# A spectral filter and an MLP in one kernel: the first DFT stage of batches 2 to 7 on quarters of the TensorE array

## The chip, the cores and the metric

The kernel runs on one core of a Trainium2 chip. The core has five engines that run side by side and wait for each other by semaphores: PE (TensorE, matmuls; PEld is its loading of weights), DVE (VectorE), ACT (ScalarE), POOL (GpSimd) and SP (SyncE, here used only to issue DMAs). Matmul results land in PSUM, which has eight banks of 128 partitions x 512 fp32 values; ACT and DVE copy them out to SBUF ("evacuate" them). The metric is the device time of one execution in microseconds (us); lower is better.

## The reference

Two operators follow each other. The first filters each of 8 batches of 3008 rows x 256 channels in the frequency domain; the second is an MLP with the snake activation.

```python
X = np.fft.rfft(x, axis=1)
F = (filt_r + 1j * filt_i)[None, :, :]
y = np.fft.irfft(X * F, n=x.shape[1], axis=1)
...
h = y.reshape(B * S, D) @ w_in          # 24064 x 256 by 256 x 2048
s = np.sin(alpha * h)
g = h + s * s / (alpha + 1e-09)
out = g @ w_out                         # 2048 x 256
```

## The kernel before, in words

**The transform.** 3008 = 47 x 64. The row index is split as n = 64 n1 + n2 with n1 < 47 and n2 < 64, and the DFT is made in two matmul stages, with their inverses behind. The first stage (`first`, tile pa) is a DFT of length 47 over n1: for each n2, 47 rows of x are contracted into 24 frequencies s, real and imaginary, thus 48 outputs. Since one such matmul would fill little of the 128x128 array, two are laid together: the chunk of x has 94 partitions, 47 values of n1 by two halves h of n2, and the weight table `wf_t` (94 x 96) is block-structured with the same 47x48 table for both halves and zeros between. A chunk `ch` holds 8 values of n2 in each half and all 256 channels; one matmul (L181) takes two of them, 512 columns. So a batch has 4 chunks of 4 matmuls. Each writes its own PSUM tile pa, which is copied as fp16 into `t1_h` (L184, by `evac`); after a chunk's fourth copy a DMA on SP's queue writes the 96 rows to DRAM (tile d1, L186).

Behind it, `load_t2` reads d1 back with n2 and the real and imaginary part on the partitions (tile t, POOL's queue), `forward` (tile pb) makes the second DFT, ACT copies it to xf, SP's queue makes a copy xs with its halves exchanged, DVE multiplies by the filter (`product`, `cross`: tiles p and xs), `inverse` (tile pc) goes back, its result g is written to DRAM (d2), read back (t4) and `last` (tile pd) yields y. Batch 0 goes by another path ahead of the main loop; batches 1 to 7 go by this one.

**The MLP.** The main loop runs over 48 chunks of up to 512 rows of y, each in 8 steps. In a step `hidden` makes two tiles ph (two accumulating matmuls each, L541). ACT takes the cosine of each (L545), DVE combines cosine and ph into v (L546). `project` then contracts the v of the chunk before with w_out, 8 matmuls of 256 columns (tile po, L560), and ACT copies po out (L568).

**The order is written out by hand.** Every piece of the transform of batch b is put into a list with a place in steps (`put(at, ...)`, where z = 48 b), the list is sorted, and `slot` calls the pieces that have come due between the step's two ph and its eight po, or after the po. Pieces with matmuls (pe=True) are spread: one per slot, unless they are late. Each engine works through its instructions in the order in which they were issued.

**PSUM.** Three pools share the eight banks: `fps` (2 banks, tag "f") serves pa, pb, pc and pd; `hps` (4 banks, tag "h") serves ph; `ops` (2 banks) serves po. A new tile waits for the evacuation of what lay in its bank before. For ph, that is DVE's v.

**evac.** `flip` counts evacuations modulo 3; without a given engine two of three go to ACT (L160) and one to DVE (L162).

**Loads of x.** `load_x` puts a chunk of x with one DMA on POOL's queue into one of four buffers (L141); it converts fp32 to fp16 on the way. From batch 2 on it also waits for the latest v (`marks["snake"]`).

Lines by tile, as the profile names them: pa L181, pb L201, pc L232, pd L254 (L343 for batch 0), ph L541, po L560, cosine L545, v L546, copies by ACT L160 and by DVE L162, xs and p L221, L215 and L222, g the copies of pc. L366 (`inverse_table`) builds a table at the start with transposes that write 64 of the 128 partitions in turn: lhsT has 64 columns there. L292, L377 and L431 belong to the start too.

Of the kernel before, what the change touches and what calls it, by code (L numbers as in the profile page):

```python
# [9 lines left out]
FP16 = mybir.dt.float16  # L10
FP32 = mybir.dt.float32
# [7 lines left out]
B, S, C = 8, 3008, 256  # L19
DFF = 2048  # L20
N1, N2 = 47, 64
NS, NQ = 24, 64
NR = 2 * N1
NK = 4 * NS
FUSED = 1


def dft_tables():

    n1, n2 = np.arange(N1), np.arange(N2)  # L30
    s, q = np.arange(NS), np.arange(NQ)
    ph = 2 * np.pi * np.outer(n1, s) / N1
    w = np.stack([np.cos(ph), -np.sin(ph)], 1)
    wf = np.zeros((N1, 2, 2, NS, 2))
    wi = np.zeros((2, NS, 2, N1, 2))
    v = np.stack([2 * np.cos(ph), -2 * np.sin(ph)], 0)
    v[0, :, 0], v[1, :, 0] = 1.0, 0.0
    for h in range(2):
        wf[:, h, :, :, h] = w
        wi[:, :, h, :, h] = v.transpose(0, 2, 1) * (8.0 / S)  # L40

    kap = np.where(q[:, None] < 32, s + N1 * q[:, None], s + N1 * (95 - q[:, None]))
    sg = np.where(q < 32, 1.0, -1.0)[:, None]
    th = 2 * np.pi * n2[:, None, None] * kap / S
    c, sn = np.cos(th), np.sin(th)
    d = np.zeros((2, N2, NS, 2, NQ))
    d[0, :, :, 0] = c.transpose(0, 2, 1)
    d[1, :, :, 0] = sn.transpose(0, 2, 1)
    d[0, :, :, 1] = (-sn * sg).transpose(0, 2, 1)
    d[1, :, :, 1] = (c * sg).transpose(0, 2, 1)  # L50
    f16 = np.float16
    wf, wi = wf.reshape(N1 * 2, 2, NS, 2), 2 * wi.reshape(2, NS, 2, NR)
    wf0, wi0 = np.zeros((96, 2, 2, 32)), np.zeros((2, 2, 32, NR))
    wf0[:NR, :, :, :NS] = wf.transpose(0, 1, 3, 2)
    wi0[:, :, :NS] = wi.transpose(0, 2, 1, 3)
    d = d.reshape(128, NS, 128).astype(f16)
    e = d.transpose(2, 1, 0) * f16(0.125)
    return (wf.reshape(NR, NK).astype(f16), wi.reshape(NK, NR).astype(f16), d,
            wf0.reshape(96, 128).astype(f16), wi0.reshape(128, NR).astype(f16), e)


# [1 line left out]
def kernel(  # L63
# [8 lines left out]
    out: bass.AP,  # L72
):
    nc = tc.nc
    wf_host, wi_host, d_host, wf0_host, wi0_host, e_host = dft_tables()
    wf_dram = nc.inline_tensor(wf_host, name="wf_tbl")
    wi_dram = nc.inline_tensor(wi_host, name="wi_tbl")
    d_dram = nc.inline_tensor(d_host, name="d_tbl")
# [8 lines left out]
    def after(ins, other):  # L87

        tc.add_manual_dep(ins.ins, other.ins.name, mybir.DependencyInfo(
            mybir.DependencyClass.Sync, mybir.DependencyReason.DATA), reason="order of loads")  # L90

    def pool(name, bufs, space=None):
        kw = {} if space is None else {"space": space}
        return ctx.enter_context(tc.tile_pool(name=name, bufs=bufs, **kw))

    cpool = pool("consts", 1)
    xpool = pool("xp", 4)
# [8 lines left out]
    fps = pool("fps", 2, PSUM)  # L106
    hps = pool("hps", 4, PSUM)
    ops = pool("ops", 2, PSUM)

    wf_t = cpool.tile([NR, NK], FP16)  # L110
    t1_h = [cpool.tile([128, 16, C], FP16, name=f"t1_h{i}") for i in range(2)]
    t4_a = cpool.tile([128, 2, 16, C], FP16)
    t4_h = [t4_a[:, i] for i in range(2)]
# [11 lines left out]
    for h in range(2):  # L125
        nc.sync.dma_start(out=x32[:, 4 * C * h:4 * C * h + 4 * C],
                          in_=bass.AP(tensor=x.tensor, offset=x.offset + 4 * h * C, ap=[[32 * C, 96], [1, 4 * C]]))
# [8 lines left out]
    marks = {}  # L136

    def load_x(b, ch):
        xt = xpool.tile([NR, 8, C], FP16, name=f"x_{b}_{ch}", tag="x")
        for n0, n in [(0, 8)] if b or ch < 3 else [(0, 4), (4, 4)]:  # L140
            ins = nc.gpsimd.dma_start(  # L141
                out=xt[:, n0:n0 + n],
                in_=bass.AP(tensor=x.tensor, offset=x.offset + (b * S + ch * 8 + n0) * C,
                            ap=[[32 * C, NR], [C, n], [1, C]]),
            )
        if b == 0:
            marks["x", ch] = ins
        if b == 1:
            marks["x1", ch] = ins
            after(ins, marks["w_in"])  # L150
        if b > 1:
            after(ins, marks["snake"])
        return xt

    flip = [0]
# [1 line left out]
    def evac(dst, src, on_act=None):  # L157
        flip[0] = (flip[0] + 1) % 3
        if flip[0] if on_act is None else on_act:
            marks["act"] = nc.scalar.copy(out=dst, in_=src)  # L160
        else:
            marks["dve"] = nc.vector.tensor_copy(out=dst, in_=src)  # L162

    class Spectral:

        def __init__(self, b):
# [5 lines left out]
            self.x, self.t2, self.t4, self.xf, self.xs, self.p = {}, {}, {}, {}, {}, {}  # L172
            self.fused = b >= FUSED

        def load_x(self, ch):
            self.x[ch] = load_x(self.b, ch)

        def first(self, i):
            ch, j = divmod(i, 4)
            ps = fps.tile([128, 512], FP32, name=f"pa_{self.b}_{i}", tag="f")  # L180
            marks["pe"] = nc.tensor.matmul(out=ps[0:NK, :], lhsT=wf_t, rhs=self.x[ch][:, 2 * j:2 * j + 2, :],  # L181
                                           start=True, stop=True)
            r0 = 8 * (ch % 2)
            evac(t1_h[ch // 2][0:NK, r0 + 2 * j:r0 + 2 * j + 2, :], ps[0:NK, :])  # L184
            if j == 3:
                nc.sync.dma_start(out=self.d1_rows[:, 8 * ch:8 * ch + 8, :],   # L186
                                  in_=t1_h[ch // 2][0:NK, r0:r0 + 8, :])

        def load_t2(self, g):
            self.t2[g] = t2pool.tile([128, 6, C], FP16, name=f"t2_{self.b}_{g}", tag="t2")  # L190
            for p in range(2):
                a0 = p * NS + 6 * g
                nc.gpsimd.dma_start(out=self.t2[g][64 * p:64 * p + 64, :, :],  # L193
                                    in_=self.d1[a0:a0 + 6, :, :].rearrange("s n c -> n s c"))
# [69 lines left out]
    id32 = cpool.tile([16, 16], FP32)  # L264
    nc.scalar.dma_start(out=id32, in_=id32_dram.ap())

    x0 = [xpool.tile([NR, 8, C], FP16, name="x_0_0", tag="x")] + [load_x(0, ch) for ch in range(1, 4)]
    nc.gpsimd.dma_start(out=d_t, in_=d_dram.ap())
    id16 = cpool.tile([128, 128], FP16)
    nc.gpsimd.dma_start(out=id16, in_=id16_dram.ap())  # L270
# [25 lines left out]
    for g in range(2):  # L296
        gs = slice(12 * g, 12 * g + 12)
        for k, filt in enumerate((filt_r, filt_i)):
            for q in range(2):
                if (g, k, q) == (0, 1, 1):  # L300
# [3 lines left out]
                    out=f_t[k][64 * k + 32 * q:64 * k + 32 * q + 32, gs, :],  # L304
                    in_=bass.AP(tensor=filt.tensor, offset=filt.offset + off,
                                ap=[[N1 * C, 32], [step, 12], [1, C]]))
# [89 lines left out]
    for i in range(16):  # L396
        own, tag = (fps, "f") if i % 3 == 2 else (hps, "h")
        ps = own.tile([128, 512], FP32, name=f"pa_0_{i}", tag=tag)
        nc.tensor.matmul(out=ps, lhsT=wf0_t[0:NR], rhs=x0[i // 4][:, 2 * (i % 4):2 * (i % 4) + 2, :],
                         start=True, stop=True)  # L400
# [62 lines left out]
    for g in range(6):  # L463
        own, tag = (t2pool, "t2") if g < 3 else (gpool, "g")
# [3 lines left out]
        ins = nc.sync.dma_start(out=w_in32[g][1], in_=w_in_v[:, :, js])  # L468
        if g == 0:
            after(ins, marks["filt", 1, 0])  # L470
        marks["w_in"] = ins
    nc.sync.dma_start(out=wf_t, in_=wf_dram.ap())
    nc.sync.dma_start(out=wi_t, in_=wi_dram.ap())
    w_out32 = vpool.tile([128, 16, C], FP32, name="w_out32", tag="v")
    for jb in range(0, 16, 8):
        ins = nc.sync.dma_start(out=w_out32[:, jb:jb + 8],
                                in_=moe_w_out[128 * jb:128 * jb + 1024].rearrange("(b p) c -> p b c", p=128))
# [120 lines left out]
    def put(at, fn, *args, pe=False):  # L598
        pending.append((at, len(pending), pe, fn, args))
# [6 lines left out]
    for b in range(1, B):  # L606
        s = s1 if b == 1 else Spectral(b)
        z = 48 * b
        if b > 1:
            for ch in range(4):  # L610
                put(22 + 4 * ch if b == 2 else z - 92 + 7 * ch, s.load_x, ch)
        for i in range(16):
            put(6.9 + 0.35 * i if b == 1 else 37 + 0.63 * i if b == 2 else z - 67 + 0.66 * i, s.first, i, pe=True)
        for g in range(4):
            put(12.5 if b == 1 else 47 if b == 2 else z - 56, s.load_t2, g)
        for u in range(12):
            inv = 24 + 1.21 * u if b == 1 else 59 + 2.1 * u if b == 2 else z - 40.8 + 2.3 * u
            fwd = inv - (6 if b == 1 else 6)
            put(fwd, s.forward, u, pe=True)
            put(fwd + (0.5 if b == 1 else 1.5), s.product, u)  # L620
            if s.fused:
                put(fwd + (4 if b == 1 else 4.5), s.cross, u)
            put(inv, s.inverse, u, pe=True)
        for ch in range(4):
            put(z - (9.5 if b == 1 and ch < 3 else (10.5, 10.5, 10.5, 3)[ch]), s.load_t4, ch)
        for u in range(16):
            put(z + (u - (5 if b == 1 else 6.5) if u < 4 else 2 * u - 9), s.last, u, pe=True)
# [59 lines left out]
```

## Time and profile before

| what | value |
|---|---|
| three runs | 786.86, 786.45, 785.05 us; median 786.45 |
| the profiled execution's own time | 783.39 us |
| its span, from the first to the last instruction | 781.6 us |
| granted TensorE clock in it | 1.0 |
| DVE L546, v | 768 of 671 ns, 482.8 us busy |
| ACT L545, cosine | 768 of 591 ns, 411.1 us busy |
| PE L560, po | 3008 of 272 ns, 389.4 us busy |
| PE L541, ph | 1536 of 374 ns, 388.0 us busy |
| ACT L160, copies of pa | 77 of 584 ns |
| DVE L162, copies of pa | 35 of 681 ns |
| PEld L181, loads of wf_t | 112 of 123 ns |
| POOL L141, loads of x | 32 issues of 540 ns; 30 of them with 376 KB, 5.0 us to landing |

The first stage of batch 2 lies at 109 to 130 us of the span, that of batch 3 at 187 to 208, then at 282 to 303, 374 to 395, 469 to 490 and 560 to 581. In these six stretches, 129.4 us in all, DVE was busy for 108.5 us and ACT for 105.4.

How to read it: a row gives line, engine, operation, out<-in, shape and count, then busy time and mean length of one, then the engine's idle time ahead of these instructions with what ended it. A matmul's record runs from its start to the modelled arrival of its last result, and the next matmul starts well before that; so records overlap, and the time that a matmul holds the engine is seen in the distance of starts. In the timeline the columns are start, length to the end of the merged group, engine, line and what is done.

### The profile page before, as it was taken

The numbers are of one execution on the slowest core, as the hardware profiler recorded it, in microseconds if no ns is written. First come the engines' busy times: TensorE is split into PE (matmuls) and PEld (weight loads), VectorE is DVE, ScalarE is ACT, GpSimd is POOL, SyncE is SP. The second block draws the span as 40 slices with busy tenths as digits, with TensorE's granted clock in tenths as the row PEclk, the third lists the DMA queues.
The fourth block names the chain that finished last, engine by engine and source line by source line (L and its number), as shares of the span: only waits on it lengthen the run. The fifth ranks groups of instructions, "written<-read, shape, count | busy, mean of one in ns | idle before, by whom it ended". The sixth has DMA issues, their size and how long they took to land.

```text
span 781.6 us, 16646 instructions
## 1 busy us (share of the span) xinstructions
PE 771.7 (99%) x5799; PEld 535.1 (68%) x5799; DVE 653.0 (84%) x1163; ACT 617.7 (79%) x1213; POOL 114.7 (15%) x192
## 2 busy tenths in 40 slices
PE   8999999999999999999999999999999999999997
PEld 4757767676667767676667766766666776766666
DVE  7887997899779997899878998789977899777773
ACT  5798988888878887888878888788887887777664
POOL 6456354200020001100020000200002000000001
PEclk9999999999999999999999999999999999999999
DMA  9946676754655446645474454736465232421111
GB/s 222 284 105 165 142 160 189 160 124 116 195 143 107 112 117 191 149 112 105 134 220 93 106 130 124 222 79 134 102 175 163 68 99 76 122 58 28 41 42 55
DMA packets 86683, 100.99 MB, mean 129 GB/s; under 512 B 14924, under 2 KB 74322, under 8 KB 86600
## 3 DMA queue, kind: packets, MB, share of 16 engines
q1 hardware_dynamic: 74525, 71.01, 32.5%
q0 software_dynamic: 11776, 28.80, 18.5%
q8 instruction: 45, 0.74, 0.4%
q14 instruction: 38, 0.31, 0.1%
q10 hardware_dynamic: 299, 0.13, 0.1%
HBM read 55.72 MB, written 46.66 MB: 131 GB/s over the span
## 4 chain that ended last, share of the span: by engine, by line
PE 94%; DVE 2%; DMA 1%; ACT 1%; issue 1%; POOL 1%; SPq 0%; POOLq 0%; ACTq 0%
PE po L560 41%; PE ph L541 40%; PE pa L181 3%; PE pd L254 2%; PE pb L201 2%; PE pc L232 2%; DVE v L546 1%; DMA id<-id 1%; PE pc L453 1%; PE pb L431 1%; PE pd L343 0%; PE warm L377 0%; POOL x L141 0%; ACT cos_all L545 0%; ACT t_h L160 0%
## 5 line engine op out<-in xcount | busy, mean ns | idle before, releaser
L546 DVE SCALAR_TENSOR_TENSOR v<-cos_all,ph 128x512 f16<-128x512 f32 (+1 forms) x768 | 482.8, 671 | 108.4 <-ACT cos_all L545 105.2
L545 ACT ACTIVATE cos_all<-ph 128x512 f32<-128x512 f32 (+1 forms) x768 | 411.1, 591 | 94.1 <-PE ph L541 93.3
L560 PE MATMUL po<-w,v 128*128 128x256 f16 x3008 | 389.4, 272 | 0.0
L541 PE MATMUL ph<-y,w 128*128 128x512 f16 (+1 forms) x1536 | 388.0, 374 | 0.7 <-DVE v L546 0.6
L560 PEld LDWEIGHTS <-v 128*128 128x128 f16 x3008 | 288.3, 98 | 77.7 <-issue 1.5
L541 PEld LDWEIGHTS <-w 128*128 128x128 f16 x1536 | 147.8, 98 | 104.5 <-issue 3.9
L568 ACT COPY o<-po 128x512 f32<-128x512 f32 (+1 forms) x97 | 55.7, 574 | 20.6 <-PE po L560 14.1
L592 POOL DMA_DIRECT2D out_dram<-o x69 | 36.0, 529 | 209.7 <-ACT o L568 208.9
L193 POOL DMA_DIRECT2D t<-d x56 | 36.4, 662 | 171.7 <-DMA out_dram<-o 131.7
L204 ACT CAST xf<-pb 128x512 f16<-128x512 f32 x84 | 49.8, 593 | 11.8 <-PE pb L201 10.7
L141 POOL DMA_DIRECT2D x<-in_x_dram x32 | 17.2, 540 | 265.9 <-PE pc L232 164.0
L160 ACT CAST t_h<-pa 96x512 f16<-96x512 f32 x77 | 45.0, 584 | 8.4 <-PE pa L181 8.2
L160 ACT CAST y<-pd 128x376 f16<-128x376 f32 (+1 forms) x83 | 39.9, 481 | 8.2 <-PE pd L254 4.4
L254 PEld LDWEIGHTS <-t_a 96*128 96x128 f16 x448 | 31.4, 97 | 18.6 <-issue 0.4
L181 PE MATMUL pa<-x,wf_t 94*96 94x512 f16 x112 | 42.5, 381 | 0.7 <-ACT t_h L160 0.4
L160 ACT CAST g<-pc 128x512 f16<-128x512 f32 x59 | 35.0, 592 | 8.6 <-PE pc L232 8.0
L222 DVE TENSOR_TENSOR p<-p,xs 128x512 f16<-128x512 f16 x84 | 35.7, 425 | 2.9
L254 PE MATMUL pd<-wi_t,t_a 96*128 96x94 f16 x448 | 37.1, 204 | 0.0
L221 DVE TENSOR_TENSOR xs<-xs,filt_t 128x512 f16<-128x512 f16 x84 | 35.0, 417 | 0.5 <-DMA xs<-xf 0.5
L215 DVE TENSOR_TENSOR p<-xf,filt_t 128x512 f16<-128x512 f16 x84 | 35.0, 417 | 0.3 <-PE pc L232 0.3
L201 PE MATMUL pb<-t,d_t 128*128 128x256 f16 x168 | 32.1, 272 | 0.0
L232 PE MATMUL pc<-p,e_t 128*128 128x256 f16 x168 | 32.1, 273 | 0.0
(64 smaller groups left out, 284.4 us busy)
## 6 DMA issues: line engine op xcount, KB each, us to landing
x<-in_x_dram POOLq DMA_DIRECT2D x30, 376.0 KB, 5.0
d<-t_h SPq DMA_DIRECT2D x28, 384.0 KB
t<-d POOLq DMA_DIRECT2D x56, 192.0 KB, 4.4
xs<-xf SPq DMA_DIRECT2D x168, 64.0 KB
d<-g SPq DMA_DIRECT2D x56, 192.0 KB
t_a<-d SPq DMA_DIRECT2D x28, 384.0 KB
out_dram<-o SPq DMA_DIRECT2D x92, 80.0 KB
w_out<-in_moe_w_out_dram SPq DMA_DIRECT2D x2, 1024.0 KB
```

The costliest lines, as they stand in the source:

```text
L160: marks["act"] = nc.scalar.copy(out=dst, in_=src)
L181: marks["pe"] = nc.tensor.matmul(out=ps[0:NK, :], lhsT=wf_t, rhs=self.x[ch][:, 2 * j:2 * j + 2, :], start=True, stop=True)
L193: nc.gpsimd.dma_start(out=self.t2[g][64 * p:64 * p + 64, :, :], in_=self.d1[a0:a0 + 6, :, :].rearrange("s n c -> n s c"))
L201: nc.tensor.matmul(out=ps[:, i, :], lhsT=d_t[:, s, :], rhs=self.t2[s // 6][:, s % 6, :], start=True, stop=True)
L204: nc.scalar.copy(out=self.xf[u], in_=ps)
L232: nc.tensor.matmul(out=ps[:, i, :], lhsT=e_t[:, 2 * w + i, :], rhs=pt[:, i, :], start=(k == 0), stop=(k == len(pr) - 1))
L254: nc.tensor.matmul(out=psv[:, i, :], rhs=wi_t, start=True, stop=True, lhsT=t4_h[ch // 2][0:NK, n0 % 16 + i, cb * 128:cb * 128 + 128])
L541: nc.tensor.matmul(out=ps[:, 0:n], lhsT=w1[:, cb, jb * 128:jb * 128 + 128], rhs=y_cols[:, cb, c0:c0 + n], start=(cb == 0), stop=(cb == 1))
L545: nc.scalar.activation(out=cs[:, 0:n], in_=ps[:, 0:n], func=AFT.Sin, bias=float(np.pi / 2))
L546: marks["snake"] = nc.vector.scalar_tensor_tensor(out=v[k][:, jb, 0:n], in0=cs[:, 0:n], scalar=-1.0, in1=ps[:, 0:n], op0=ALU.add, op1=ALU. ...
L560: nc.tensor.matmul(out=pso[k][:, t % 2, :], lhsT=v[k][:, jb, 128 * t:128 * t + 128], rhs=w2[:, jb, :], start=(jb == 0), stop=(jb == 15))
L568: nc.scalar.copy(out=o[:, i0:t % 2 + 1, :], in_=pso[k][:, i0:t % 2 + 1, :])
```

## The change

Batches 2 to 7 get a new first stage, `first_tiled`; batch 1 keeps `first`. A chunk of x now lies on two groups of partitions, n1 = 0 to 46 of half h = 0 on partitions 0 to 46 and those of h = 1 on 64 to 110, by two DMAs with 47 rows each. The weight table `wt_t` holds the plain 47x48 table twice, at rows 0 and 64, with 64 columns (16 of them zero). A matmul takes 47 rows and 64 columns, a quarter of the array: h picks the half of the rows, c the half of the columns, and so the half of the PSUM partitions that is written. Each still has 512 columns of x (two values of n2, all channels). A chunk has 8 of them instead of 4, in two rounds q of four. The two halves h write different PSUM tiles. The first round takes both banks of `fps`, the second takes two of the four banks of `hps`, which until then served ph alone. The four copies of a chunk now cover all 128 partitions; h = 0 goes to ACT, h = 1 to DVE. Two DMAs on SP's queue write d1 in place of one, with the same content at the same place.

Issue moves too: a whole chunk with its 8 matmuls, 4 copies and 2 DMAs is one piece of the list, where before each of its 4 matmuls was a piece of its own.

```diff
+    wt = np.zeros((2, 64, 64))
+    wt[:, :N1, :2 * NS] = w.reshape(N1, 2 * NS)
...
-        xt = xpool.tile([NR, 8, C], FP16, name=f"x_{b}_{ch}", tag="x")
+        xt = xpool.tile([128, 8, C], FP16, name=f"x_{b}_{ch}", tag="x")
+        if b >= TILED:
+            for h in range(2):
+                ins = nc.gpsimd.dma_start(
+                    out=xt[64 * h:64 * h + N1],
+                    in_=bass.AP(tensor=x.tensor, offset=x.offset + (b * S + 32 * h + ch * 8) * C,
+                                ap=[[64 * C, N1], [1, 8 * C]]))
+                after(ins, marks["snake"])
+            return xt
+        xt = xt[0:NR]
...
+        def first_tiled(self, ch):
+            r0 = 8 * (ch % 2)
+            for q in range(2):
+                own, tag = (hps, "h") if q else (fps, "f")
+                ps = [own.tile([128, 512], FP32, name=f"pa_{self.b}_{ch}_{q}_{h}", tag=tag) for h in range(2)]
+                for h in range(2):
+                    for c in range(2):
+                        n = 4 * c + 2 * q
+                        nc.tensor.matmul(out=ps[h][64 * c:64 * c + 64, :], lhsT=wt_t[64 * h:64 * h + N1],
+                                         rhs=self.x[ch][64 * h:64 * h + N1, n:n + 2, :], start=True, stop=True)
+                for h in range(2):
+                    evac(t1_h[ch // 2][:, r0 + 4 * h + 2 * q:r0 + 4 * h + 2 * q + 2, :], ps[h], h == 0)
+            d1 = self.d1.rearrange("a (h n) c -> a h (n c)", h=2)
+            for c in range(2):
+                n0 = (8 * ch + 4 * c) * C
+                nc.sync.dma_start(out=d1[:, :, n0:n0 + 4 * C],
+                                  in_=t1_h[ch // 2][64 * c:64 * c + 2 * NS, r0:r0 + 8, :]
+                                  .rearrange("a (h n) c -> a h (n c)", h=2))
...
+    nc.sync.dma_start(out=wt_t, in_=wt_dram.ap())
...
-        for i in range(16):
-            put(6.9 + 0.35 * i if b == 1 else 37 + 0.63 * i if b == 2 else z - 67 + 0.66 * i, s.first, i, pe=True)
+        if b < TILED:
+            for i in range(16):
+                put(6.9 + 0.35 * i, s.first, i, pe=True)
+        else:
+            for ch in range(4):
+                put((37, 40, 42, 45)[ch] if b == 2 else z - 67 + (0, 3, 5, 8)[ch], s.first_tiled, ch, pe=True)
```

More of the change, by code (lines that the diff above doesn't have):

```diff
@@ L25 @@
 FUSED = 1
+TILED = 2
 def dft_tables():
@@ L57, in dft_tables @@
     e = d.transpose(2, 1, 0) * f16(0.125)
-    return (wf.reshape(NR, NK).astype(f16), wi.reshape(NK, NR).astype(f16), d,
+    wt = np.zeros((2, 64, 64))
+    wt[:, :N1, :2 * NS] = w.reshape(N1, 2 * NS)
+    return (wt.reshape(128, 64).astype(f16), wf.reshape(NR, NK).astype(f16), wi.reshape(NK, NR).astype(f16), d,
             wf0.reshape(96, 128).astype(f16), wi0.reshape(128, NR).astype(f16), e)
@@ L74 @@
     nc = tc.nc
-    wf_host, wi_host, d_host, wf0_host, wi0_host, e_host = dft_tables()
+    wt_host, wf_host, wi_host, d_host, wf0_host, wi0_host, e_host = dft_tables()
+    wt_dram = nc.inline_tensor(wt_host, name="wt_tbl")
     wf_dram = nc.inline_tensor(wf_host, name="wf_tbl")
@@ L110 @@
     wf_t = cpool.tile([NR, NK], FP16)
+    wt_t = cpool.tile([128, 64], FP16)
     t1_h = [cpool.tile([128, 16, C], FP16, name=f"t1_h{i}") for i in range(2)]
@@ L150, in load_x @@
             after(ins, marks["w_in"])
-        if b > 1:
-            after(ins, marks["snake"])
         return xt
@@ L265 @@
     nc.scalar.dma_start(out=id32, in_=id32_dram.ap())
-    x0 = [xpool.tile([NR, 8, C], FP16, name="x_0_0", tag="x")] + [load_x(0, ch) for ch in range(1, 4)]
+    x0 = [xpool.tile([128, 8, C], FP16, name="x_0_0", tag="x")[0:NR]] + [load_x(0, ch) for ch in range(1, 4)]
     nc.gpsimd.dma_start(out=d_t, in_=d_dram.ap())
```

## The prediction

> **What bounds the kernel now.** I read the page's first lines, then its chain, then the rows of the engines that meet in this stage.
>
> ```profile
> span 781.6 us, 16646 instructions
> PE 771.7 (99%) x5799; PEld 535.1 (68%) x5799; DVE 653.0 (84%) x1163; ACT 617.7 (79%) x1213; POOL 114.7 (15%) x192
> ...
> PE 94%; DVE 2%; DMA 1%; ACT 1%; issue 1%; POOL 1%; SPq 0%; POOLq 0%; ACTq 0%
> ...
> L181 PE MATMUL pa<-x,wf_t 94*96 94x512 f16 x112 | 42.5, 381 | 0.7 <-ACT t_h L160 0.4 <-ACT y L160 0.2
> ```
>
> TensorE (PE) is busy throughout and makes 94% of the chain that ends last, so a microsecond taken from it comes off the end, and a microsecond in which it waits is added. The stage to be changed (L181) waited only 0.7 us in all. A busy record overlaps the next one, so the price of a matmul is the distance between starts, from the timeline of PE:
>
> ```profile
> 302.23 0.38 PE L181 MATMUL pa<-x,wf_t 94*96 94x512 f16 x1
> 302.45 1.03 PE L541 MATMUL ph<-y,w 128*128 128x512 f16 x4
> ```
>
> One first-stage matmul holds PE for 302.45 - 302.23 = 0.22 us, not for the 0.38 of its record.
>
> **Removed.** Batches 2 to 7 have 6 x 16 = 96 of the 112 matmuls: 96 x 0.22 = 21.1 us of PE. With them goes most of L181's waiting; I count 0.5 of the 0.7 us.
>
> **Added on PE.** 24 chunks of 8 matmuls, each on a quarter of the array, four quarters (two halves of the rows, two of the columns) in each of two rounds. Before has no quarters, but it has halves: L366 writes the two column halves in turn (128x64). PE's timeline there:
>
> ```profile
> 13.13 0.44 PE L292 MATMUL al_bc<-part,one 128*128 128x128 bf16 x5
> ...
> 14.76 1.08 PE L366 MATMUL pse<-id,d_t 128*64 128x128 f16 x32 [0.97 <-DMA id<-id]
> 15.78 1.50 PE L431 MATMUL pb<-t_a,d_t 128*128 128x128 f16 x12
> 17.21 0.64 PE L366 MATMUL pse<-id,d_t 128*64 128x128 f16 x16
> 17.78 1.04 PE L377 MATMUL warm<-idle 128*128 128x512 f16 x4
> ```
>
> A record of 128 columns lasts 0.22 us. On the whole array (L292) four distances take 0.44 - 0.22, 0.055 each. On halves, 32 matmuls put their last start at 14.76 + 1.08 - 0.22 = 15.62: 15 distances of pairs in 0.86, 0.057 each. So two halves run in the time of one. I take it that four quarters do too: a round costs the 0.22 of one 512-column matmul, and a chunk 0.44. At the other end only two quarters run together, and a chunk costs 0.88.
>
> Then the change of shape. The last L431 starts one record (mean 0.29) before 17.28, at 16.99; the whole-array matmul after the halves starts at 17.78. In these 0.79 us lie one L431 (distance (16.99 - 15.78)/11 = 0.11) and eight pairs (at 0.055 to 0.057, 0.44 to 0.46), which leaves 0.22 to 0.24 for going in and out. I take 0.25 per chunk. Lower end: the first block's way out, 15.78 - 15.62 - 0.057 = 0.10, taken twice: 0.20. Upper end: L431 counted at 0.055, 0.30, plus one weight load of 0.11 (L366's loads last 106 to 110 ns) that four quarters might not overlap: 0.41.
>
> PE's own sum: 24 x (0.88 - 0.44 - 0.25) = 4.6 us saved (0.7 to 5.8 between the ends), 5.1 with the 0.5.
>
> **A rule against it.** The Trainium skill, "TensorE: Matmul & The Clock Gate", section "Measured speedup vs the span model", reports 3.07x, not 4x, for four row tiles of 512 columns. By that a round would cost 4 x 0.22 / 3.07 = 0.29, the 48 rounds 3.3 us more, and the change would end slower. The row shows no loss for two halves, so I keep 0.22; no row of before shows four.
>
> **Moved to the evacuations.** Before, a chunk's four results are drained one by one between other work: in batch 4's stretch (281 to 304 us, the view of the tile pa) ScalarE took 11 and VectorE 4 of the 16, the last lying outside. Now two each per chunk, in one burst: 48 and 48, some 16 copies moved to VectorE. ScalarE gets lighter and is dropped. VectorE's copies stand 0.60 us apart:
>
> ```profile
> 289.23 1.28 DVE L546 SCALAR_TENSOR_TENSOR v<-cos_all,ph 128x512 f16<-128x512 f32 x2 [0.41 <-ACT cos_all L545]
> 290.44 0.68 DVE L162 CAST t_h<-pa 96x512 f16<-96x512 f32 x1
> ```
>
> (290.44 - 289.23 = 1.21 for two.) A step is a pair of ph, eight po, and what is put between; bare it takes PE 4 x 0.216 + 8 x 0.109 = 1.74, with a chunk 1.74 + 0.69 = 2.43. VectorE needs 1.20 for the pair's two v and 1.20 for the chunk's two copies: 2.40 in 2.43. The chunk also takes two of the four banks of ph, so the next ph must wait for the v of the pair just before it. Undisturbed, that v ends 1.95 us after its pair starts (for the pair at 285.48: v from 286.74, 0.68 long, ends at 287.42), inside 2.43. So most chunks fit, with little to spare. I went through all 24 in the changed program's order. These do not fit:
>
> - Batch 2, first chunk. VectorE is behind here. On its timeline the v of the pairs at 106.26 and 108.21 stand in one block, for which the chunk, put after the second pair, has to wait:
>
> ```profile
> 109.31 3.68 DVE L546 SCALAR_TENSOR_TENSOR v<-cos_all,ph 128x512 f16<-128x512 f32 x6
> ```
>
> The first two of its six free the banks of the second round, at 109.31 + 0.68 = 109.99 and 110.59. The chunk starts at 108.21 + 0.86 + 0.13 = 109.20 (half of the 0.25 on the way in) and could start that round at 109.41; it ends 110.59 - 109.41 = 1.2 us late. I take 1.15, since the first bank lets two quarters run earlier.
> - Batch 3, second chunk. In the program's waits the second pair of the first round waits for ScalarE's copy of the first pair: both have the same bank. A record (0.38), a copy (0.58), signals, less nothing of the pair that ran: 1.0 us.
> - Batches 4 and 7, first chunk: the second pair's bank still holds a pc that VectorE copies (g, 281.91 to 282.60 in before), while the chunk is ready at 281.35 + 0.86 + 0.13 = 282.34: 0.25 each, 0.5.
> - The pc or pd that follows at once in ten or so places waits for the first copy: it comes 1.4 us after the chunk's start, and the copy, behind the cosines, ends at 1.2 to 1.5: 0.1 each, 0.9 with odd ones.
>
> Together 3.5 us. Lower end 1.5, if the two large ones shrink by half and the small ones vanish; upper end 8.4 (the rival below).
>
> **DMAs and queues.** Each x chunk is two POOL issues in place of one (24 more at 540 ns, 13 us) on a queue busy 15%, loaded over ten steps ahead; the d1 writes are two SP issues in place of one, behind whose waits the xs copies queue, used some four steps later. The last chunk's place (step z - 59) is ahead of that of the last matmul before (z - 57.1), and the t loads keep theirs (z - 56). The cover is steps of 2 us; I put them at nothing, and at one late load of 5.0 us (x's time to landing) if it were gone. The table wt_t is one more load at the start, hidden among the weights.
>
> **Sum.** 5.1 - 3.5 = 1.6 us faster: the profiled execution's 783.39 (span 781.6) would be 781.8. The median shown, 786.45, lies 3.1 above that execution; 786.45 - 1.6 = 784.9. Its bounds are 782.9 (waits 1.5) and 787.0 (change of shape at 0.34).
>
> **Rivals.** 0.2% of the median is 1.6 us, the least that a measurement here tells from none.
>
> *Slower: VectorE's burst decides.* Each chunk's two copies hold VectorE past the next pair, and in the next chunk PE waits for v. For it: 2.40 of 2.43; VectorE was busy 84%; xs and p (0.42 each) fall into some of these steps, and 2.40 + 0.80 = 3.2 does not fit. Against it: in ordinary steps the bank of a ph is needed again two steps on, 2 x 1.74 - 1.95 = 1.5 us after its v, in which VectorE catches up. With 0.35 us of waiting at each chunk (0.8 too much, somewhat over half of it taken up by the ordinary steps), 24 x 0.35 = 8.4: 8.4 - 5.1 = 3.3 slower, 789.8. It decides above 5.1 / 24 = 0.21 us per chunk.
>
> *Waits hidden.* Only 1.5 us or less is new, and the shape costs 0.20: 24 x 0.24 + 0.5 - 1.5 = 4.8 faster, 781.7. For it: L181 and L541 waited 0.7 us each in before. Against it: the shared bank and batch 2's block are in the order itself.
>
> *The array isn't shared four ways.* The change then does not do what it says: rows one after the other, +24 x 0.44 = 10.6, so 10.6 - 1.6 = 9 slower, 795.5. For it: no row of before has row halves. Against it: column halves overlap without loss.
>
> **Chances.** Forecast 0.45, hidden waits 0.20, VectorE's burst 0.27, not shared 0.08. The forecast's centre lies on the bound: I split it 0.23 faster, 0.20 same, 0.02 slower. The burst gives 0.02 to same, 0.25 to slower. Faster 0.43, same 0.22, slower 0.35. The forecast's own range is 782.9 to 787.0; to hold 8 in 10 it reaches past both neighbouring rivals by about half the spread of the runs shown (785.05 to 786.86), to 780.5 and 790.5, and leaves out the unshared array and the burst's far tail.
>
> **What would show it.** Right: the eight new matmuls of an undisturbed chunk take some 0.7 us from the first start to the next po; waits on the new line sum to about 3 us, the largest near 109 us and in batch 3's second chunk. Wrong: rounds of 0.44 rather than 0.22; a way in and out above 0.4; idle time before L541's line of several microseconds with VectorE's v as its releaser; t loads or x loads that PE waits for.

## The result and the profile after

The changed kernel takes 792.72 us (median of 4 runs, 790.62 to 793.73) where the kernel before, run beside it, takes 786.06 (785.05 to 786.86): a ratio of 1.0082 [1.0057, 1.0106], 6.7 us slower. The prediction was 784.9 with a range of 780.5 to 790.5; the time lies outside it, on the slow side. The profiled execution took 792.33 us (783.39 before). The two slowest of the four runs, 793.1 and 793.73 us, show a granted clock of 0.998 and 0.997, so the median may hold some 1 to 2 us of clock (an estimate: 0.002 or 0.003 of 791 us); the main loop of the profiled run, from which this section reads, ran at 1.0.

The head of the page, its chain, and the row of `last`'s matmuls (pd):

```profile
span 790.5 us, 16898 instructions
PE 769.8 (97%) x5895; PEld 526.0 (67%) x5895; DVE 661.2 (84%) x1180; ACT 611.5 (77%) x1196; POOL 126.5 (16%) x216
...
PE 89%; DMA 5%; DVE 3%; ACT 1%; issue 1%; SPq 0%; POOL 0%; POOLq 0%; ACTq 0%; DVEq 0%
...
L285 PE MATMUL pd<-wi_t,t_a 96*128 96x94 f16 x448 | 37.2, 205 | 8.4 <-DMA t_a<-d 8.4
```

PE is busy for 1.9 us less, and yet the span is 8.9 longer. In the chain, DMA went from 1% to 5%. The last row says where PE stood: 8.4 us ahead of pd, for loads of t4 (t_a<-d). Before, nothing stood there:

```profile
L254 PE MATMUL pd<-wi_t,t_a 96*128 96x94 f16 x448 | 37.1, 204 | 0.0
```

The new stage itself (after, groups with shapes kept apart) waited little:

```profile
L209 PE MATMUL pa<-x,wt_t 47*64 47x512 f16 x192 | 17.5, 389 | 1.3 <-ACT t_h L172 0.7 <-DVE v L578 0.7
```

Records of matmuls overlap, so I went by the distances from one matmul's start to the next, over the main loop: a part counts by as much as it makes PE's path longer, and a wait is what a distance has above the usual one between two such neighbours. This is worked out from the trace; each row is before against after.

| part of the main loop | before, us | after, us | difference |
|---|---|---|---|
| whole length | 741.3 | 749.5 | +8.1 |
| `first`, matmuls (after: batch 1 alone) | 24.6 | 3.5 | -21.1 |
| `first`, waits | 1.83 | 1.23 | -0.6 |
| 24 chunks of `first_tiled`, with waits | 0 | 19.4 | +19.4 |
| waits ahead of pd | 0.24 | 9.38 | +9.1 |
| waits ahead of ph and pc | | | +0.9 |
| the rest | | | +0.4 |

Without the line for pd the sum is -1.0 us, near the forecast's -1.6. One term that the forecast put at nothing is nearly the whole miss. It consists of six waits, one per batch from 1 to 6, whose distances are 1.92, 2.30, 1.29, 1.72, 1.44 and 1.42 us instead of 0.1 to 0.2.

**One such wait, from both queues.** PE's timeline, after:

```profile
311.00 0.81 PE L573 MATMUL ph<-y,w 128*128 128x384 f16 x4
311.65 1.04 PE L592 MATMUL po<-w,v 128*128 128x256 f16 x8
313.71 0.34 PE L285 MATMUL pd<-wi_t,t_a 96*128 96x94 f16 x4 [1.02 <-DMA t_a<-d]
313.88 0.82 PE L573 MATMUL ph<-y,w 128*128 128x384 f16 x4
```

The bracket is the time that PE stood and what ended it. When was this load issued? SP's queue holds, among others, the d1 writes (L186 before, L216 after), the writes of g (L239, L270), the t4 loads (L244, L275) and the stores of the output, in the order of the program. Its timeline in the kernel before (columns: start, length to the end of the merged group, queue, line, out<-in, count):

```profile
299.82 0.32 SPq L186 DMA_DIRECT2D d<-t_h  x1
300.23 1.63 SPq L244 DMA_DIRECT2D t_a<-d  x3
305.71 0.30 SPq L186 DMA_DIRECT2D d<-t_h  x1
...
307.46 0.33 PE L254 MATMUL pd<-wi_t,t_a 96*128 96x94 f16 x4
```

(the last line is PE's: the first pd that needs these loads) and after, with VectorE's copies of the last chunk:

```profile
302.86 4.07 SPq L624 DMA_DIRECT2D out_dram<-o  x7
306.07 1.28 DVE L174 CAST t_h<-pa 128x512 f16<-128x512 f32 x2
307.41 1.21 SPq L216 DMA_DIRECT2D d<-t_h  x2
308.72 1.84 SPq L275 DMA_DIRECT2D t_a<-d  x3
```

Before, the t4 loads of one batch stand ahead of the last d1 write of the next; the write could go out as late as 305.71 and nothing that PE needed soon stood behind it. pd started at 307.46, 7.2 us after its loads were issued. After, the order is turned round: the last chunk's d1 writes stand ahead of the t4 loads. SP is done with the stores at 306.93, waits for DVE's two copies of that chunk (they run from 306.07 to 307.35), issues two writes of 0.6 us each, and comes to the t4 loads at 308.72, 5.0 us ahead of the pd that needs them. The loads lost 1.7 us to the writes (from 306.93 and the usual gap of some 0.1 to 308.72), and PE stood for 1.02.

The loads themselves were hardly slower: worked out from the trace, the first load of a batch took 5.2 us from issue to landing before and 5.4 after (means of batches 2 to 6). They came later. Before, SP issued it 6.5 to 7.4 us ahead of pd; after, 5.0 to 5.8 us with PE's waiting counted in, 3.1 less without it (means). The writes held it for 1.3 to 2.7 us, some 2.1 on average; the other 1 us or so of lost lead is not theirs.

Batch 1 loses by the same queue, one step removed. Its t4 loads read what the writes of g (d<-g) put into d2. SP's queue, after:

```profile
115.03 1.27 SPq L216 DMA_DIRECT2D d<-t_h  x2
116.42 1.46 SPq L270 DMA_DIRECT2D d<-g  x2
121.47 1.26 SPq L275 DMA_DIRECT2D t_a<-d  x3
```

and before:

```profile
104.57 8.21 SPq L239 DMA_DIRECT2D d<-g  x4
115.05 1.45 SPq L244 DMA_DIRECT2D t_a<-d  x3
116.62 8.74 SPq L186 DMA_DIRECT2D d<-t_h  x3
```

The d1 writes of batch 2's first chunk now stand ahead of batch 1's last two writes of g, and the loads go out 6.4 us later in the span.

**The new stage itself did what it should.** Undisturbed and disturbed chunks in PE's timeline, after; x8 in one line means that nothing came between:

```profile
293.38 1.03 PE L573 MATMUL ph<-y,w 128*128 128x512 f16 x4
294.34 0.63 PE L209 MATMUL pa<-x,wt_t 47*64 47x512 f16 x8
294.89 1.05 PE L592 MATMUL po<-w,v 128*128 128x256 f16 x8
...
110.76 0.41 PE L209 MATMUL pa<-x,wt_t 47*64 47x512 f16 x4
111.64 0.40 PE L209 MATMUL pa<-x,wt_t 47*64 47x512 f16 x2 [0.46 <-DVE v L578]
112.23 0.40 PE L209 MATMUL pa<-x,wt_t 47*64 47x512 f16 x2 [0.19 <-DVE v L578]
112.57 1.05 PE L592 MATMUL po<-w,v 128*128 128x256 f16 x8
...
197.45 0.41 PE L209 MATMUL pa<-x,wt_t 47*64 47x512 f16 x2
198.53 0.62 PE L209 MATMUL pa<-x,wt_t 47*64 47x512 f16 x6 [0.68 <-ACT t_h L172]
```

Eight matmuls lie within 0.63 us though one record alone lasts 0.39. The single starts in the trace: the four quarters of a round begin 3 to 4 ns apart, the second round 0.240 us after the first began, and the next po 0.308 after the last of them (294.89 - 294.34 = 0.55 in all). The way in, from the last ph, is 0.309 where one matmul to the next takes 0.216. An undisturbed chunk lengthens PE's path by 0.651 us. If a round costs 0.216, the distance of a whole matmul, two rounds leave 0.22 for the change of shape there and back; experiment 5 tests this split. The other two examples are batch 2's first chunk (1.90 us instead of 0.65: it stands for two v) and batch 3's second (1.73: its second pair, at 198.53, starts 1.08 after the first, since both have one bank).

### The profile page after: what moved, and what is told of

It is laid out like the page before. It is cut to its first block, busy times and chain, and to the rows that moved or that the text cites. A ratio compares the mean times of both kernels' runs of the same rounds, so it can differ in the third digit from the quotient of the medians.

```text
span 790.5 us, 16898 instructions
## 1 busy us (share of the span) xinstructions
PE 769.8 (97%) x5895; PEld 526.0 (67%) x5895; DVE 661.2 (84%) x1180; ACT 611.5 (77%) x1196; POOL 126.5 (16%) x216
## 4 chain that ended last, share of the span: by engine, by line
PE 89%; DMA 5%; DVE 3%; ACT 1%; issue 1%; SPq 0%; POOL 0%; POOLq 0%; ACTq 0%; DVEq 0%
PE po L592 39%; PE ph L573 38%; DMA t_a<-d 4%; PE pd L285 3%; PE pb L232 2%; PE pc L263 2%; PE pa L209 2%; DVE v L578 2%; DMA xs<-xf 1%; PE pc L484 1%; DMA al<-in_moe_alpha_dram 1%; PE warm L408 1%; PE pb L462 1%; PE pa L193 0%; PE pd L374 0%
## 5 line engine op out<-in xcount | busy, mean ns | idle before, releaser
L147 POOL DMA_DIRECT2D x<-in_x_dram x48 | 24.4, 514 | 270.4 <-PE pc L263 170.9
L172 ACT CAST y<-pd 128x376 f16<-128x376 f32 (+1 forms) x83 | 39.9, 481 | 15.6 <-PE pd L285 11.8
L172 ACT CAST g<-pc 128x512 f16<-128x512 f32 x59 | 35.0, 592 | 10.5 <-PE pc L263 9.9
L172 ACT CAST t_h<-pa 128x512 f16<-128x512 f32 (+1 forms) x60 | 33.2, 601 | 3.1 <-PE pa L209 1.7
L174 DVE CAST t_h<-pa 128x512 f16<-128x512 f32 (+1 forms) x52 | 33.5, 682 | 0.5 <-PE pa L209 0.5
```

## The experiments

Two groups of four, each beside runs of the kernel before on the same chip: 784.56 us (783.69 to 787.18) for the first group, 784.86 (783.69 to 786.71) for the second. The theory under test, Q, is the queue: the d1 writes that now stand ahead of the t4 loads. Its rival R is the transfers: smaller pieces, more of them, so that the loads themselves take longer or stand in line behind other traffic. The times of two experiments of different groups are compared by their ratios to the kernel before.

**1. The t4 loads a step earlier.** It alters one number of the order, and leaves the writes, their size and their number.

```diff
-            put(z - (9.5 if b == 1 and ch < 3 else (10.5, 10.5, 10.5, 3)[ch]), s.load_t4, ch)
+            put(z - (9.5 if b == 1 and ch < 3 else (11.5, 11.5, 11.5, 3)[ch]), s.load_t4, ch)
```

> The changed kernel, with the t4 loads of batches 2 to 7 (first three chunks) placed at step z-11.5 instead of z-10.5, so that on SP's queue they stand ahead of the next batch's last d1 writes instead of behind them. In the changed kernel PE waited for t4 loads ahead of pd six times, 9.1 us beyond the usual distance of starts, 7.5 of it in batches 2 to 6 and 1.7 in batch 1, which this edit leaves alone. Theory Q (SP's order holds the loads): the five waits go, 792.7 - 7.5 = 785.2. Rival R (the d1 writes in rows of 2 KB load the DMA engines, and the t4 loads are slow wherever they stand): only the step of lead (1.7 us) is gained where the transfer is still slow; the loads take as long from issue to first pd as before, and waits of 0 to 0.6 remain at each.

Measured: 783.35 us (782.93 to 785.82), ratio to before 0.9987 [0.9975, 0.9999]. From the changed kernel's 1.0082 that is 0.0095 less, 7.5 us. SP's timeline has the loads ahead of the writes again, and pd's row is left with one wait:

```profile
303.30 1.25 SPq L275 DMA_DIRECT2D t_a<-d  x3
304.65 1.20 SPq L216 DMA_DIRECT2D d<-t_h  x2
...
L285 PE MATMUL pd<-wi_t,t_a 96*128 96x94 f16 x448 | 37.1, 204 | 1.6 <-DMA t_a<-d 1.6
```

By the distances, the waits ahead of pd went from 9.38 to 1.79 us, 7.6 less, as much as the time. The one left is batch 1's, whose t4 loads the edit doesn't touch: they have step 38.5, and batch 2's first chunk now brings its two d1 writes at step 37, ahead of them and of the last writes of g.

**2. The other way round: the last chunk later.** The t4 loads stay; the chunk whose writes stand ahead of them is put behind.

```diff
-                put((37, 40, 42, 45)[ch] if b == 2 else z - 67 + (0, 3, 5, 8)[ch], s.first_tiled, ch, pe=True)
+                put((37, 40, 42, 45)[ch] if b == 2 else z - 67 + (0, 3, 5, 9.5)[ch], s.first_tiled, ch, pe=True)
```

> The changed kernel, with the last first-stage chunk of batches 3 to 7 1.5 steps later (z-57.5 for z-59), so that its d1 writes stand behind the t4 loads on SP's queue; the t4 loads keep their place. Theory Q: the five waits of batches 2 to 6 go, 792.7 - 7.5 = 785.2, perhaps 0.5 less exactly since the chunk now meets other work. Rival R: the d1 writes now run at the same time as the t4 loads, which stay slow: at most half of the waits goes, 789 or more.

Measured: 783.45 us (782.39 to 786.93), 0.9988 [0.9975, 1.0002], the same as the first. Again pd has one wait, of 1.8 us:

```profile
L285 PE MATMUL pd<-wi_t,t_a 96*128 96x94 f16 x448 | 37.2, 204 | 1.8 <-DMA t_a<-d 1.8
```

(The chunk in its new place brings a wait of its own: 0.9 us ahead of pb, for loads of t.) In both experiments all transfers of the changed kernel are there, in the same number and size, and five of six waits are gone; the order on the queue is the cause. R falls as an account of what the change lost, since the loads took 5.4 us after and 5.2 before. But it has a share in what the two edits win back: ahead of the writes the first load of a batch lands in 4.3 us (both experiments, means of batches 2 to 6), 1.1 less than behind them.

**3. The t4 loads on another queue.** POOL issues the first three of each batch instead of SP.

```diff
-            nc.sync.dma_start(out=t4_h[ch // 2][0:NK, r0:r0 + 8, :],
+            (nc.sync if ch == 3 else nc.gpsimd).dma_start(out=t4_h[ch // 2][0:NK, r0:r0 + 8, :],
```

> The changed kernel, with the first three t4 loads of each batch issued by POOL instead of SP at the same place in the steps. Nothing is moved in time and the d1 writes stay as they are; only the queue differs. Theory Q: all six waits go, batch 1's too, unless POOL itself is held by an older wait: 792.7 - 9.1 = 783.6. Rival R (transfers) and rival L (the shorter steps alone leave the loads too little lead): the waits stay, 792 or so.

Measured: 787.93 us (786.25 to 788.95), 1.0044 [1.0027, 1.0061]: about 3 us gained of some 9, so partly a miss. The waits of batches 2 to 6 are gone but for 0.4 us at batch 2's, and batch 1's grew to a distance of 2.88. The row of pd, and POOL's timeline at the place shown above and at batch 1's loads:

```profile
L285 PE MATMUL pd<-wi_t,t_a 96*128 96x94 f16 x448 | 37.3, 205 | 2.8 <-DMA t_a<-d 2.8
...
302.72 1.52 POOL L275 DMA_DIRECT2D t_a<-d  x3 [19.63 <-PE ph L573]
...
119.60 1.54 POOL L275 DMA_DIRECT2D t_a<-d  x3 [7.76 <-DMA d<-g]
```

The loads go out at 302.72, and no d1 write is ahead of them. In batches 3 to 6 they go out 7.0 to 9.2 us ahead of pd, so their place in the steps leaves lead enough, and rival L falls too. In batch 1 POOL had to wait for the writes of g, which are still behind d1 writes on SP's queue, and the first load then took 5.2 us to land instead of 3.9.

The rest lies in the clock, as far as the profiled run shows. Right behind batch 1's wait the granted clock falls to half (the 0.51 in this row, the view of 125.4 to 128.9 us; then come the DMA engines' share and GB/s):

```profile
125.40:128.90 3.50, 3.50 (x20) 2.27 (x18) 0.99 (x2) 1.90 (x4) 1.37 (x3) 0.51 1.04 345
```

From the pd at 124.88 to the second ph behind it, at 129.29, PE needs 4.41 us; the changed kernel, at a clock of 1.0, needs 2.75 for the same matmuls. These 1.7 us and the 0.9 by which batch 1's wait is longer than in experiment 1 are most of the 3.1 between the two profiled runs (786.25 and 783.18). The three other runs show clocks of 0.995 to 0.997, where those of the kernel before have 0.999 to 1.0. What brought the clock down was not tried.

**4. What the quarters are worth.** Experiment 1 with the same burst, the same banks and copies, but as four whole matmuls of 94 x 96 as before (and one d1 write and one x load per chunk, as before).

```diff
-                    for c in range(2):
-                        n = 4 * c + 2 * q
-                        nc.tensor.matmul(out=ps[h][64 * c:64 * c + 64, :], lhsT=wt_t[64 * h:64 * h + N1],
-                                         rhs=self.x[ch][64 * h:64 * h + N1, n:n + 2, :], start=True, stop=True)
+                    n = 4 * h + 2 * q
+                    nc.tensor.matmul(out=ps[h][0:NK, :], lhsT=wf_t, rhs=self.x[ch][:, n:n + 2, :],
+                                     start=True, stop=True)
...
```

> As the first of these runs (t4 ahead), but without quarters: a chunk is four matmuls of 94x96 as before the change, still issued as one piece into four banks with two copies each on ACT and DVE, x and d1 by one DMA each. It tells the tiles from the burst. By the prediction's terms a chunk costs PE 0.88 instead of 0.44 + 0.25 = 0.69 (0.66 in the trace of the changed kernel): 24 x 0.19 to 0.22 = 4.6 to 5.3 us more than the first run, 790 to 790.5, if the quarters run together as read; with the same waits for banks. Rival (the quarters bring nothing, the burst alone costs): the same time as the first run or less.

Measured: 785.43 us (784.45 to 787.2), 1.0005 [0.9994, 1.0017]; 2.1 us above experiment 1 by the medians, 1.4 by the ratios, 2.6 by the main loops of the two profiled runs. Of the 4.6 to 5.3 us that were expected, 1.4 to 2.6 came. An undisturbed chunk takes 0.865 us of PE, 4 x 0.216, against 0.651. So the quarters save 0.214 per chunk, 5.1 us over 24. About a third to a half of it is seen in the time. The rest is in the trace: the waits of the chunks are 2.2 us instead of 3.6 (whole matmuls are slower, so the second round likely finds its banks free more often), and with one d1 write per chunk batch 1's wait ahead of pd is nearly gone (0.36 instead of 1.79 in all). 5.1 - 1.4 - 1.4 = 2.3, within the measured 1.4 to 2.6: more than half of what the quarters save is spent in waits that come with them.

**5. What the change of shape is worth.** Experiment 1 with the two rounds as separate pieces, half a step apart, so that PE changes shape twice as often.

```diff
-        def first_tiled(self, ch):
+        def first_tiled(self, ch, q):
...
-                put((37, 40, 42, 45)[ch] if b == 2 else z - 67 + (0, 3, 5, 8)[ch], s.first_tiled, ch, pe=True)
+                [put((37, 40, 42, 45)[ch] + 0.5 * q if b == 2 else z - 67 + (0, 3, 5, 8)[ch] + 0.5 * q, s.first_tiled, ch, q, pe=True) for q in range(2)]
```

> As the first run (t4 ahead), with the two rounds of each chunk put half a step apart, so that the eight po of a step lie between them. Same matmuls, copies and DMAs, but the array changes its shape twice per chunk instead of once. The trace of that run has an undisturbed chunk at 0.65 us, of which two rounds of 0.22 leave 0.22 for one way in and out. If that is the price: 24 x 0.22 = 5.2 us more than the first run, less what the gentler demand for banks gives back (its waits sum to 3.5 us, 1 to 2 of it might go): ratio to the kernel before 0.9987 + 0.004 to 0.0067 = 1.003 to 1.005. Rival (the rest of the 0.65 is not the change of shape but the start of any burst, the four whole-array matmuls of the fourth run being the same burst without it): no more than 1 us added.

Measured: 786.67 us (785.86 to 788.31), 1.0026 [1.0017, 1.0036], by the ratios 0.0039 or 3.1 us above experiment 1, just under the expected 1.003 to 1.005. PE's timeline of one piece:

```profile
290.83 0.59 PE L573 MATMUL ph<-y,w 128*128 128x512 f16 x2
291.36 0.41 PE L209 MATMUL pa<-x,wt_t 47*64 47x512 f16 x4
291.70 1.05 PE L592 MATMUL po<-w,v 128*128 128x256 f16 x8
```

One round lengthens PE's path by 0.436 us, from single starts. Two rounds in one visit take 0.651, so the second one adds 0.215, and what is left of the 0.436 for the change there and back is 0.22. Two such pieces cost 0.87, as much as four whole matmuls (0.865). A round saves two whole matmuls' 0.43 less its own 0.216, thus 0.216, and a change of shape costs just that. Of the 24 x 0.22 = 5.3 us more, the chunks' waits gave back 1.6 (2.0 instead of 3.6 in all).

**6. Batch 2 later.** Experiment 1, with batch 2's chunks behind batch 1's t4 loads and out of VectorE's block of v.

```diff
-                put((37, 40, 42, 45)[ch] if b == 2 else z - 67 + (0, 3, 5, 8)[ch], s.first_tiled, ch, pe=True)
+                put((39, 41, 43, 45)[ch] if b == 2 else z - 67 + ((0, 3, 5, 8) if b == 3 else (0, 3, 5, 8))[ch], s.first_tiled, ch, pe=True)
```

> As the first run (t4 ahead), with batch 2's first-stage chunks at steps 39, 41, 43, 45 instead of 37, 40, 42, 45: the first one now stands behind batch 1's t4 loads (38.5) on SP's queue, and two steps past the stretch in which VectorE is behind. By the trace of the first run PE waits 1.8 us for batch 1's t4 and 1.0 us in that chunk for banks that VectorE frees: both go, 2.8 us less than the first run, ratio to before 0.9987 - 0.0036 = 0.995. Rival for the bank wait (not VectorE's being late but the chunk's own two copies): only the 1.8 goes, 0.9964.

Measured: 780.98 us (780.2 to 783.01), 0.9954 [0.9939, 0.9969]; by the ratios 0.0033 or 2.6 us below experiment 1, most of the 2.8 that left PE's path at these two places (the last wait ahead of pd, 1.79, and 0.99 at the first chunk, which took 1.64 in experiment 1 and now takes 0.652). The row of pd has no idle time left:

```profile
L285 PE MATMUL pd<-wi_t,t_a 96*128 96x94 f16 x448 | 37.1, 204 | 0.0
```

**7. All four chunks moved to where banks are free.** Experiment 1, with places such that no round gets one bank twice.

```diff
-                put((37, 40, 42, 45)[ch] if b == 2 else z - 67 + (0, 3, 5, 8)[ch], s.first_tiled, ch, pe=True)
+                put((38.5, 41, 43, 45)[ch] if b == 2 else z - 67 + ((0.5, 2.5, 5, 8) if b == 3 else (0.5, 2.5, 5, 8))[ch], s.first_tiled, ch, pe=True)
```

> As the run before, and the other named waits avoided by place: chunks of batch 2 at 38.5, 41, 43, 45, those of batches 3 to 7 at z-67 + 0.5, 2.5, 5, 8, which in the built program gives the two tiles of a round separate banks in all 24 chunks (in the changed kernel batch 3's second chunk has one bank for both, 1.08 us) and puts the first chunk behind the step's po, past VectorE's copy of pc in batches 4 and 7 (0.34 each). From the first run: 1.8 + 1.0 + 1.08 + 0.68 = 4.6 us less, 0.9987 - 0.0058 = 0.993 of before. Rival (VectorE is the bound in this stage and a wait taken away at one place returns at the next): no less than 0.996.

Measured: 779.72 us (779.16 to 780.01), 0.9933 [0.9916, 0.995], 5.1 us below the kernel before and, by the ratios, 0.0054 or 4.2 us below experiment 1: the version that beats both. Groups by shape:

```profile
L285 PE MATMUL pd<-wi_t,t_a 96*128 96x94 f16 x448 | 37.1, 204 | 0.0
...
L209 PE MATMUL pa<-x,wt_t 47*64 47x512 f16 x192 | 15.6, 388 | 0.0
```

Both rows are free of waits. By the distances the 24 chunks cost 16.6 us in all, of which 24 x 0.651 = 15.6 is the bare work; three chunks still cost 0.2 to 0.4 more than that.

**8. A control.** The kernel before with experiment 1's edit of the t4 loads, to see whether the earlier load is worth something by itself.

> Control: the kernel before the change, with its t4 loads of batches 2 to 7 at z-11.5 as in the first run. There the last d1 write stands behind the t4 loads anyway and PE hardly waits for pd's loads (0.24 us in all). Theory Q: no change, ratio 0.998 to 1.002. Rival (an earlier t4 load is worth something by itself): faster by as much as the first run gained over the changed kernel, 0.990.

Measured: 784.94 us (783.6 to 787.05), 1.0006 [0.9994, 1.0017]: no change. What experiment 1 gained was therefore the changed kernel's own loss.

## Why the prediction was wrong

**The step that failed** is the paragraph on DMAs and queues: "the d1 writes are two SP issues in place of one, behind whose waits the xs copies queue, used some four steps later. The last chunk's place (step z - 59) is ahead of that of the last matmul before (z - 57.1), and the t loads keep theirs (z - 56). The cover is steps of 2 us; I put them at nothing". It saw that the last chunk moved earlier and looked at what the chunk's own data need next: the t loads. It did not ask which *other* transfers on SP's queue the writes moved past. Counted in steps, the last chunk of a batch stands at z - 59; written with the z' = z - 48 of the batch before it, that is z' - 11, and the first three t4 loads of that batch before stand at z' - 10.5. In the kernel before, the last matmul stood at z - 57.1 = z' - 9.1, behind them. Both places are in the code, so the crossing could have been read without a run. It cost 9.1 us where nothing was written, and experiments 1 and 2 take 7.5 of it back, each by undoing the crossing from one side. In batch 1 the chunk at step 37 passed the writes of g as well, on which the t4 loads at step 38.5 wait.

The price of "one late load, 5.0 us, if the cover were gone" was also wrong in kind: the cover went once in each of six batches, with PE idle for 1.0 to 2.0 us each time, and not once.

**Sizes that held.**
- Removed: 21.1 us forecast, 21.1 measured; L181's waits 0.5 forecast, 0.6 measured.
- A round of four quarters: 0.22 forecast, 0.215 to 0.24 measured. The rival of an array that isn't shared four ways falls: the four starts are 3 to 4 ns apart, and the next round follows 0.240 us after the first. The Trainium skill's 3.07x for four row tiles ("TensorE: Matmul & The Clock Gate", section "Measured speedup vs the span model") would have meant, by the prediction's estimate, 0.29 per round; that row of the page is for tiles of 32 rows and not for quarters, the trace shows no such loss here, and the measurement decides.
- Change of shape: 0.25 forecast, with 0.20 to 0.41 as bounds; 0.22 measured, from the visits of one and of two rounds together.
- Waits of the chunks: 3.5 us forecast, 3.7 measured. By place: batch 2's first chunk 1.15 forecast, 1.25 measured; batch 3's second 1.0 and 1.08; the first chunks of batches 4 and 7 0.25 and 0.34 each. The forecast's last 0.9, for a pc or pd behind some ten chunks, did not show there. That the sum came so near is luck: three chunks that were not named waited 0.37, 0.31 and 0.13. Outside the chunks pc and ph waited 0.9 longer, 0.84 of it just ahead of batch 2's first chunk.

**Rivals.** VectorE's burst does not decide: 7 of 24 chunks waited at all, ph lost 0.5 us more than before, while DVE's busy time went from 653.0 to 661.2 us. "Waits hidden" falls by the same 3.7. The slower side came by a mechanism that stood among the signs to look for ("t loads or x loads that PE waits for"), though for the t4 loads, and had no rival or price of its own. That the prediction's other terms come out within 0.6 us in sum is read from the table of distances. Experiment 1 agrees with it, as far as one wait of 1.8 us and quicker loads allow: its ratio of 0.9987 lies beside the forecast's 784.9 / 786.45 = 0.9980.

Two things stay open: what lowers the clock in experiment 3, and what took the 1 us or so of the loads' lead that the writes did not take.

## What to carry to other kernels

In an order written by hand, a piece that is moved takes its DMAs with it: for each queue, list what they are moved past, other batches' pieces included, because here two writes that waited for their copies held every load behind them. List also what the data of those loads wait for on the same queue. Work on quarters of the array saved whole rounds here but paid 0.22 us for the change of shape each time PE went there and back, so keep the rounds together: two in a row saved 0.21 us per visit and one alone saved nothing. And when a stage needs several PSUM banks at once, go through the order for each visit to see which banks it gets and who must empty them: moving the chunks' places was worth 4.2 us here on top of the mended queue, the last queue wait among it.

## What was not expected of the hardware

The d1 writes cost SP's queue more each, though each carries half: the median issue of a write took 597 ns after (192 KB, 48 rows with two runs of 2 KB each) against 316 ns before (384 KB, 96 rows with one run of 4 KB each). So a chunk holds the queue for 1.21 us instead of 0.32, which is most of the 1.7 us that the t4 loads lost. The price of an issue did not follow the bytes of the transfer; which property of its shape sets it, was not tried.
